# A fused attention and gMLP kernel: a smaller scratch tile in the opening's pool, and GpSimd's sums of weight blocks two column tiles later

## The chip, the cores and the metric

The kernel runs on one core of a Trainium2 chip. The metric is the device time of one execution in microseconds. Engines carry their names in the profile: PE is TensorE, DVE is VectorE, ACT is ScalarE, POOL is GpSimd, SP is SyncE, which here only issues DMAs.

## The reference

One token matrix x of 2048 rows and 512 columns is normalised row by row, and two branches work on the result. All is float32.

```python
xn = _layernorm(x, axis=-1)
s = _A_ref(xn, A_wqkv, A_wo)
g = _silu(_B_ref(xn, B_w_in, B_w_sp, B_b_sp, B_w_out))
return x + s * g
```

Branch A is attention with 32 heads of 16 columns. Each row looks at itself and at seven earlier rows, two apart (window 8, dilation 2), with a softmax over these eight, and the result is multiplied by wo. Branch B is a gMLP: z = gelu(xn @ w_in) with 1792 columns. The second half of z is normalised by row and mixed along the rows by the 2048 x 2048 matrix w_sp, with b_sp added. The result is multiplied by the first half and projected by w_out.

## The kernel before

**Numbers.** TensorE's products are made in fp32r, each operand split into a high and a low part, so one product is three matmuls: high by high, high by low, low by high. A split (`split`, L190 to L193) is an ACT copy for the high part and a DVE subtraction for the low one.

**The opening (L240 to L498).** The product xn @ wqkv is made in three groups of 512 columns, `pair(g, j0)` (L421 to L437) doing two row tiles of 128 at a time: 12 matmuls for a row tile, an ACT copy into a tile `stage`, and from it one store to the DRAM buffer `qkv_d`, 24 stores in all. Group 0 holds the columns that subs 0 and 1 of the attention read, group 2 the last ones. The first six row tiles are transposed by TensorE. Tiles 6 to 15 are fetched already transposed (`fetch_cols`, L255), and a column tile (`column_tile`, L272 to L278) is normalised on DVE by two products (L275) with rows of mean and scale, which come back by DRAM (`rows_out`, `rows_in`: the tile mr), then copied by ACT (L278); `low_x` (L229) makes its low part on DVE. The pow that makes 1/sqrt is on POOL (`rows_ready`, L259 to L262).

**The sums of weight blocks.** Part of the mixing by w_sp uses sums of its blocks. `block_sums` (L389 to L397) loads two tiles of two blocks, adds four times, and stores both tiles to `sums_d`, which the mixing reads much later. Five such sums for the second half are made in the opening by POOL alone, loads, adds and stores (`early_sums`, L410, called at L472 and L473 behind column tile 10 and ahead of column tile 11). Their tiles are t2 tiles. A dependence without a semaphore (NOSYNC, L394) puts their loads behind the last pow in POOL's order.

**Pools of SBUF tiles.** Left of the memory lie whole (the tile BIG), wts, then early (the opening's rows and columns) and, once early is closed, att (the attention's tiles, L513). On the right lie raws, const, then tmp (L88: t2, the stage tiles t35, the tile tz of L350, zpad) and, once tmp is closed (L506), wide (L507: the tiles of the later stages). A pool that is opened on bytes of a closed one waits for the last use of that one.

**The attention (L515 to L664)** works in 16 units: eight subs of four heads, two halves of the rows each. For a unit k, q and v are loaded from `qkv_d` (L536, L537, L545). Two steps per unit are made on DVE: products of q with the eight shifted k (L556), their sums (L563), maximum and shift (L580, L581), an exponential on ACT (L586), the normalisation (L592 to L594), products with v (L600), a first fold on POOL (`first_fold`, L610), two more on DVE (L615, L616), a transpose (L623), and four stores to `o_d` (L626). All have the lowest priority but are chained in their own order.

**The rest** is TensorE's main line: z1 and z2, the two halves of xn @ w_in (L678 to L680, L705 to L707), the mixing g (L795), the projection b by w_out (L1018 to L1020 with the names b), stored to `b_d`, and the attention's projection s by wo (the same lines with the names s), for which `o_d` is loaded (L778) and split. Then the gate is loaded (sg, L1040), goes through silu (L1063), and is multiplied by s (L1073) and added to x (L1075, L1078).

**What sets the order.** The framework's planner lists the instructions of each engine by priority and by its own estimate of when they can run; what `pin` wraps keeps the program's order. Each engine and each issuing queue then goes through its list in order.

Of the kernel before, what the change touches and what calls it, by code (L numbers as in the profile page):

```python
# [11 lines left out]
F32 = mybir.dt.float32  # L12
F32R = mybir.dt.float32r
AF = mybir.ActivationFunctionType
ALU = mybir.AluOpType
AX = mybir.AxisListType

P = 128
S, D, F = 2048, 512, 1792
# [3 lines left out]
NT = S // P  # L23
# [6 lines left out]
HT = NT // 2  # L30
# [21 lines left out]
SYNC = mybir.DependencyInfo(mybir.DependencyClass.Sync, mybir.DependencyReason.DATA)  # L52
NOSYNC = mybir.DependencyInfo(mybir.DependencyClass.NoSync, mybir.DependencyReason.DATA)
# [4 lines left out]
def kernel(  # L58
# [13 lines left out]
    nc = tc.nc  # L72
    pins = [True]

    def pin(ins):
        return tc.keep_in_program_order(ins) if pins[0] else ins
# [12 lines left out]
    tmp = opened.__enter__()  # L89
# [16 lines left out]
    nhalf = raws.tile([P, 1], F32, name="nhalf")  # L106
# [12 lines left out]
    def xn_at(j):  # L119
        return planes[:, FB - KB :, j, 0], planes[:, FB - KB :, j, 1]  # L120
# [22 lines left out]
    def blocks(t, n=KB):  # L143
        return t.rearrange("p (k q) -> p k q", k=n)

    def t2(name, dt=F32, tag="t2", bufs=4):
        return tmp.tile([P, 2 * D], dt, tag=tag, name=name, bufs=bufs)

    def t35(name, dt=F32, wide=False):
        return tmp.tile([P, 2 * GC], dt, tag="t35", name=name, bufs=3)[:, : 2 * GC if wide else FH]  # L150
# [3 lines left out]
    def mm(name):  # L154
        return ps.tile([P, 512], F32, tag=f"bank{next(turn)}", name=name)
# [3 lines left out]
    def weight_pair(name):  # L159
        i = next(slot)  # L160
        return (
            wts.tile([P, 512], F32R, tag=f"whi{i}", name=name + "h"),
            wts.tile([P, 512], F32R, tag=f"wlo{i}", name=name + "l"),
        )

    def fetch(src, n, name):
        raw = raws.tile([P, 512], F32, tag="raw", name=name + "r", bufs=RAW)
        pin(nc.sync.dma_start(raw[:, :n], src))
        return raw
# [25 lines left out]
    def load_x(j):  # L195
        xt = t2(f"x_{j}")[:, :D]
        pin(nc.sync.dma_start(xt, xr[j]))
        return xt

    def stats_x(j, xt):  # L200
        st = const.tile([P, 6], F32, tag="st", name=f"st_{j}", bufs=4)
        pin(nc.vector.bn_stats(st, xt))
        pin(nc.vector.bn_aggr(mvx[:, j], st))
        if j >= JC:
            rstd_x(j)

    def rstd_x(j):
        pin(nc.vector.tensor_scalar(mvx[:, j, 1:2], mvx[:, j, 1:2], EPS, None, op0=ALU.add))
        pin(nc.gpsimd.tensor_tensor(mvx[:, j, 1:2], mvx[:, j, 1:2], nhalf, op=ALU.pow))
# [4 lines left out]
    def normal_x(j, xt):  # L214
        if j < JC:
            pin(nc.vector.tensor_scalar(xt, xt, mvx[:, j, 0:1], None, op0=ALU.subtract))
        else:
            pin(normalise(xt, xt, mvx[:, j]))

    def turned_x(j, xt):  # L220
        pt = mm(f"xt_{j}")
        for i in range(KB):
            pin(nc.tensor.transpose(pt[:, i * P : (i + 1) * P], xt[:, i * P : (i + 1) * P], ident))
        pin(nc.scalar.activation(xn_at(j)[0], blocks(pt), AF.Copy))
        return pt

    def low_x(j, pt):
        hi, lo = xn_at(j)
        pin(nc.vector.tensor_tensor(lo, blocks(pt), hi.bitcast(F32), op=ALU.subtract))  # L229
# [12 lines left out]
    rows = {}  # L242
# [16 lines left out]
    def rows_ready(j0, j1):  # L259
        v = mvx[:, j0:j1, 1]  # L260
        pin(nc.vector.tensor_scalar(v, v, EPS, None, op0=ALU.add))
        return pin(nc.gpsimd.tensor_tensor(v, v, nhalf.to_broadcast([P, j1 - j0]), op=ALU.pow))  # L262

    def rows_in(j0, j1):
        mr = ep.tile([P, 4, 2, P], F32, tag="mr", name=f"mr_{j0}", bufs=2)[:, : j1 - j0]
# [6 lines left out]
    def column_tile(j):  # L272
        xv = cols[j].rearrange("p (k q) -> p k q", k=KB)
        for a, op in ((0, ALU.subtract), (1, ALU.mult)):
            pin(nc.vector.tensor_tensor(  # L275
                xv, xv, rows[j][:, a].unsqueeze(1).to_broadcast([P, KB, P]), op=op
            ))
        pin(nc.scalar.activation(xn_at(j)[0], blocks(cols[j]), AF.Copy))  # L278

    warm = mm("warm")  # L280

# [5 lines left out]
    first = []  # L287

    def opening(wg):
        def high(k):  # L290
            hi, lo = weight_pair(f"wqkv_0_{k}")
            pin(nc.scalar.activation(hi, raw[k], AF.Copy))
            wg[k] = hi, lo

        def low(k, eng):
            pin(eng.tensor_tensor(wg[k][1], raw[k], wg[k][0].bitcast(F32), op=ALU.subtract))

        left = [12, 12]

        def times(j, *kab):  # L300
            for k, a, b in kab:
                pin(nc.tensor.matmul(
                    first[j], xn_at(j)[a][:, k], wg[k][b],
                    start=left[j] == 12, stop=left[j] == 1,
                ))
                left[j] -= 1

        x = [load_x(0)]
        raw = [fetch(wqkv[:, 0, 0, :], GC, "wqkv_0_0")]
        x.append(load_x(1))  # L310
        raw += [fetch(wqkv[:, 0, k, :], GC, f"wqkv_0_{k}") for k in (1, 2)]
        raw.append(t35("wqkv_0_3r")[:, :GC])
        pin(nc.sync.dma_start(raw[3], wqkv[:, 0, 3, :]))
        x.append(load_x(2))
        stats_x(0, x[0])
        high(0)
        normal_x(0, x[0])
        low(0, nc.vector)
        p = turned_x(0, x[0])
        stats_x(1, x[1])  # L320
        low_x(0, p)
        high(1)
        normal_x(1, x[1])
        rstd_x(0)
        low(1, nc.vector)
        high(2)
        low(2, nc.gpsimd)
        keep_warm(2)
        first.append(mm("qkv_0_0"))
        times(0, (0, 0, 0), (0, 0, 1))  # L330
        p = turned_x(1, x[1])
        high(3)
        stats_x(2, x[2])
        low(3, nc.gpsimd)
        times(0, (0, 1, 0), (1, 0, 0), (1, 1, 0), (1, 0, 1), (2, 0, 0), (2, 1, 0))
        low_x(1, p)
        normal_x(2, x[2])
        rstd_x(1)
        first.append(mm("qkv_0_1"))
        times(1, *[(k, 0, 0) for k in range(KB - 1)], (0, 0, 1), (1, 0, 1))  # L340
        times(0, (3, 0, 0), (3, 1, 0), (2, 0, 1))
        p = turned_x(2, x[2])
        times(1, (3, 0, 0), *[(k, 1, 0) for k in range(KB)], (2, 0, 1))
        times(0, (3, 0, 1))
        times(1, (3, 0, 1))
        x += [load_x(j) for j in range(3, OPEN)]
        for j in range(OPEN, OPEN + 4):
            fetch_rows(j)
        raw1 = [fetch(wqkv[:, 1, k, :], GC, f"wqkv_1_{k}") for k in range(3)]
        raw1.append(t2("wqkv_1_3r", tag="tz", bufs=1)[:, :D])  # L350
        pin(nc.sync.dma_start(raw1[3], wqkv[:, 1, 3, :]))
        for j in range(3, OPEN):
            xt = x[j]
            stats_x(j, xt)
            low_x(j - 1, p)
            normal_x(j, xt)
            if j - 1 < JC:
                rstd_x(j - 1)
            first.append(mm(f"qkv_0_{j - 1}"))
            left.append(12)  # L360
            times(j - 1, *[(k, 0, i) for i in range(2) for k in range(KB)])
            p = turned_x(j, xt)
            times(j - 1, *[(k, 1, 0) for k in range(KB)])
            row_stats(OPEN + j - 3)
        low_x(OPEN - 1, p)
        for j in range(10, 13):
            fetch_rows(j)
        for j in range(6, 10):
            fetch_cols(j)
        rows_ready(6, 9)  # L370
        rows_out(6, 9)
        return raw1
# [16 lines left out]
    def block_sums(a, i, tile_=None, eng=nc.vector, loads=nc.sync, stores=nc.scalar):  # L389
        top, low = [(tile_ or t4)(f"s{n}_{a}_{i}") for n in "ab"]  # L390
        for t, r in ((top, 0), (low, HT)):
            ins = loads.dma_start(t, w_sp[2 * a : 2 * a + 2, r + i].rearrange("c p t -> p c t"))
            if tile_:
                tc.add_manual_dep(ins.ins, rows_known.ins.name, NOSYNC, reason="rows first")  # L394
        added([top[:, 0], top[:, 1], low[:, 0], low[:, 1]], eng)
        for r, t in enumerate((top, low)):
            stores.dma_start(sums_d[a, r, i], t)  # L397
# [12 lines left out]
    def early_sums(a, i):  # L410
        block_sums(a, i, early_tile, nc.gpsimd, nc.gpsimd, nc.gpsimd)
# [45 lines left out]
    pair(1, 0)  # L457
    for j in range(13, NT):
        row_stats(j)
    rows_known = rows_ready(13, NT)  # L460
    column_tile(8)
    low_x(7, cols[7])
    fetch_cols(12)
# [5 lines left out]
    column_tile(10)  # L469
    low_x(9, cols[9])  # L470
    pair(1, 4)
    for i in range(HT - 3):  # L472
        early_sums(1, i)  # L473
    for j in range(11, NT):
        if j + 2 < NT:
            fetch_cols(j + 2)
        column_tile(j)
        low_x(j - 1, cols[j - 1])
        if j % 2:
            pair(0, j - 5)  # L480
# [574 lines left out]
    for i in range(0, NT, 2):  # L1055
        j0 = rows_of[i]
# [67 lines left out]
```

## Time and profile before

| what | value |
|---|---|
| median of 3 runs | 753.29 us (751.03 to 753.71) |
| the profiled execution | 751.32 us |
| its span, first to last instruction | 749.5 us |
| PE busy | 697.5 us (93%) |
| DVE busy | 614.3 us (82%) |
| ACT busy | 288.8 us (39%) |
| POOL busy | 154.4 us (21%) |
| mean granted clock of TensorE | 0.967 |

A line of a timeline gives the start, the busy time, the engine and line, the tiles written and read, and in brackets how long the engine had been idle and what released it. PE's matmuls overlap, so their distance counts and not their length. SPq, ACTq are the issuing sides of these engines, and DMA lines are transfers. Tile names are shown without their first numbers.

### The profile page before, as it was taken

How to read it: one execution, taken by the hardware profiler on the slowest of the kernel's cores; microseconds unless marked ns; L12 is line 12 of the kernel's file. 1: busy time of each engine (PE TensorE's matmuls, PEld its weight loads, DVE VectorE, ACT ScalarE, POOL GpSimd, SP SyncE). 2: the span in 40 equal slices, each digit the busy share in tenths (PEclk: the TensorE clock that was granted, in tenths of full speed). 3: DMA queues.
4: the chain of work that ended last, by engine and by line, in shares of the span. 5: the costliest groups of instructions: out<-in, count | busy, mean ns of one | idle time of the engine just before them, and what ended most of it. 6: DMA issues, size and time to landing. Idle time of an engine off the chain costs nothing.

```text
span 749.5 us, 9288 instructions
## 1 busy us (share of the span) xinstructions
PE 697.5 (93%) x3084; PEld 578.8 (77%) x3084; DVE 614.3 (82%) x882; ACT 288.8 (39%) x460; POOL 154.4 (21%) x150
## 2 busy tenths in 40 slices
PE   8989999999999999799999999999999999990474
PEld 7867888888889888588888888888888888880364
DVE  6768310159998999989999999999999999979845
ACT  4422332333424548665345443333434421131222
POOL 3155730000122463421111112111110121221000
PEclk9989999999999999899999999999999999996698
DMA  8798994399998736769997866938778264453568
GB/s 278 224 294 286 297 336 127 102 329 410 363 370 318 234 111 204 224 179 294 373 301 265 277 225 218 313 128 256 234 236 297 74 227 162 164 177 99 151 241 334
DMA packets 109633, 182.38 MB, mean 243 GB/s; under 512 B 10256, under 2 KB 50448, under 8 KB 109584
## 3 DMA queue, kind: packets, MB, share of 16 engines
q1 hardware_dynamic: 66528, 125.55, 50.9%
q10 hardware_dynamic: 40176, 45.75, 17.4%
q0 software_dynamic: 2880, 10.49, 3.9%
q8 instruction: 24, 0.39, 0.2%
q14 instruction: 25, 0.20, 0.1%
HBM read 122.42 MB, written 59.32 MB: 242 GB/s over the span
## 4 chain that ended last, share of the span: by engine, by line
PE 73%; DVE 13%; DMA 8%; issue 2%; ACT 2%; SPq 1%; POOL 0%; DVEq 0%; ACTq 0%
PE g L795 36%; PE qkv L381 4%; PE qkv L380 4%; PE qkv L379 4%; PE z L679 3%; PE z L678 3%; PE z L680 3%; PE z L707 3%; PE z L706 3%; PE z L705 3%; DMA sg<-b_d 3%; DMA ol<-o_d 2%; DVE pr L556 2%; PE b L1019 2%; PE b L1018 2%
## 5 line engine op out<-in xcount | busy, mean ns | idle before, releaser
L610 POOL TENSOR_TENSOR pv<-pv 128x1024 f32<-128x1024 f32 x29 | 69.7, 2403 | 440.4 <-DVE pv L600 440.4
L556 DVE TENSOR_TENSOR pr<-k,q 128x2048 f32<-128x2048 f32 x32 | 73.6, 2299 | 1.3 <-DMA q<-qkv_d 1.2
L600 DVE TENSOR_TENSOR pv<-v,lg 128x2048 f32<-128x2048 f32 x32 | 73.2, 2287 | 0.6
L563 DVE TENSOR_REDUCE lg<-pr 128x128 f32<-128x2048 f32 x32 | 72.9, 2278 | 0.0
L427 ACT ACTIVATE stage<-qkv 128x512 f32<-128x512 f32 x36 | 21.2, 595 | 50.0 <-PE qkv L381 49.9
L1018 PE MATMUL s<-BIG 128*128 128x512 f32 x16 | 7.3, 459 | 27.8 <-ACT BIG L191 27.8
L192 DVE TENSOR_TENSOR w_4l<-w_4r,w_4h 128x512 fp32r<-128x512 f32 x1 | 0.7, 692 | 34.6 <-ACT w_4h L191 34.6
L275 DVE TENSOR_TENSOR xT<-xT,mr 128x512 f32<-128x512 f32 x20 | 18.0, 899 | 11.8 <-DMA mr<-mv_d 9.3
L1029 ACT ACTIVATE bt<-b 128x512 f32<-128x512 f32 x16 | 9.4, 599 | 43.6 <-PE b L1020 39.3
L1018 PEld LDWEIGHTS s<-BIG 128*128 128x128 f32 x16 | 3.5, 220 | 29.0 <-ACT BIG L191 28.3
L707 PE MATMUL z<-w_0h,BIG 128*128 128x512 f32 x64 | 25.0, 391 | 0.0
L706 PE MATMUL z<-w_0l,BIG 128*128 128x512 f32 x64 | 25.0, 391 | 0.0
L705 PE MATMUL z<-w_0h,BIG 128*128 128x512 f32 x64 | 24.9, 389 | 0.0
L726 ACT ACTIVATE zt<-zt,nmz,mvz 128x896 f32<-128x896 f32 x16 | 18.1, 1136 | 11.7 <-POOL nmz L722 11.7
L615 DVE TENSOR_TENSOR pv<-pv 128x512 f32<-128x512 f32 x32 | 21.8, 681 | 0.0
L707 PE MATMUL z<-w_1h,BIG 128*128 128x384 f32 x64 | 21.5, 336 | 0.0
L705 PE MATMUL z<-w_1h,BIG 128*128 128x384 f32 x64 | 21.5, 335 | 0.0
L706 PE MATMUL z<-w_1l,BIG 128*128 128x384 f32 x64 | 21.4, 335 | 0.0
L381 PE MATMUL qkv<-wqkv_0h,BIG 128*128 128x512 f32 x43 | 17.5, 407 | 3.2 <-DVE BIG L229 3.2
L795 PE MATMUL g<-ws_0h,BIG 128*128 128x512 f32 x52 | 20.2, 389 | 0.0
L795 PE MATMUL g<-ws_1h,BIG 128*128 128x512 f32 x52 | 20.2, 389 | 0.0
L795 PE MATMUL g<-ws_2h,BIG 128*128 128x512 f32 x52 | 20.2, 389 | 0.0
(471 smaller groups left out, 2282.8 us busy)
## 6 DMA issues: line engine op xcount, KB each, us to landing
qkv_d<-stage ACTq DMA_DIRECT2D x24, 512.0 KB, 5.0
k<-qkv_d SPq DMA_DIRECT2D x16, 704.0 KB, 5.3
v<-qkv_d SPq DMA_DIRECT2D x16, 704.0 KB, 3.9
z_d<-z1t ACTq DMA_DIRECT2D x14, 512.0 KB
zl<-z_d SPq DMA_DIRECT2D x12, 512.0 KB, 5.9
tr<-t_d SPq DMA_DIRECT2D x12, 384.0 KB, 5.9
x<-in_x SPq DMA_DIRECT2D x16, 256.0 KB, 4.5
sa<-in_w_sp SPq DMA_DIRECT2D x8, 512.0 KB
```

What stands on the lines that cost most here:

```text
L379: nc.tensor.matmul(pq, xh[:, k], wh, start=k == 0, stop=False)
L380: nc.tensor.matmul(pq, xh[:, k], wl, start=False, stop=False)
L381: nc.tensor.matmul(pq, xl[:, k], wh, start=False, stop=k == KB - 1)
L556: line(nc.vector.tensor_tensor(pr, taps(ks[u], j0), qb.unsqueeze(1).to_broadcast([P, W, NJ * CS]), op=ALU.mult))
L563: line(nc.vector.tensor_reduce(lgs[u][:, :, j0 * HS : (j0 + NJ) * HS], pr.rearrange("p w (i d) -> p w i d", d=DH), axis=AX.X, op=ALU.add,))
L600: line(nc.vector.tensor_tensor(pv.rearrange("p w (i d) -> p w i d", d=DH), taps(vs[u], j0).rearrange("p w (i d) -> p w i d", d=DH), lgs[u] ...
L610: eng.tensor_tensor(pv[:, 0:4], pv[:, 0:4], pv[:, 4:8], op=ALU.add)
L705: nc.tensor.matmul(pz, xh[:, k], wh, start=k == 0, stop=False)
L706: nc.tensor.matmul(pz, xh[:, k], wl, start=False, stop=False)
L707: nc.tensor.matmul(pz, xl[:, k], wh, start=False, stop=k == KB - 1)
L795: nc.tensor.matmul(pg, z[a], w[b], start=start and i == 0, stop=stop and i == 2, skip_group_check=seeded)
L1018: nc.tensor.matmul(pp[:, cols], hi, wh, start=k == 0, stop=False)
```

## The change

The helper `t2` takes a width, and the tile tz takes half of the bytes it had. The sums' loop moves from ahead of column tile 11 to behind column tile 12, and its loads wait by a semaphore (SYNC) for the last DVE product of that column tile instead of standing behind the pow. `rows_ready` and `column_tile` are changed only in what they return.

```diff
-    def t2(name, dt=F32, tag="t2", bufs=4):
-        return tmp.tile([P, 2 * D], dt, tag=tag, name=name, bufs=bufs)
+    def t2(name, n=2, tag="t2", bufs=4):
+        return tmp.tile([P, n * D], F32, tag=tag, name=name, bufs=bufs)
...
     def column_tile(j):
         xv = cols[j].rearrange("p (k q) -> p k q", k=KB)
         for a, op in ((0, ALU.subtract), (1, ALU.mult)):
-            pin(nc.vector.tensor_tensor(
+            done = pin(nc.vector.tensor_tensor(
                 xv, xv, rows[j][:, a].unsqueeze(1).to_broadcast([P, KB, P]), op=op
             ))
         pin(nc.scalar.activation(xn_at(j)[0], blocks(cols[j]), AF.Copy))
+        return done
...
-        raw1.append(t2("wqkv_1_3r", tag="tz", bufs=1)[:, :D])
+        raw1.append(t2("wqkv_1_3r", 1, tag="tz", bufs=1))
...
             if tile_:
-                tc.add_manual_dep(ins.ins, rows_known.ins.name, NOSYNC, reason="rows first")
+                tc.add_manual_dep(ins.ins, turned.ins.name, SYNC, reason="columns first")
...
-    for i in range(HT - 3):
-        early_sums(1, i)
     for j in range(11, NT):
         if j + 2 < NT:
             fetch_cols(j + 2)
-        column_tile(j)
+        turned = column_tile(j)
+        if j == 12:
+            for i in range(HT - 3):
+                early_sums(1, i)
         low_x(j - 1, cols[j - 1])
```

More of the change, by code (lines that the diff above doesn't have):

```diff
@@ L261, in rows_ready @@
         pin(nc.vector.tensor_scalar(v, v, EPS, None, op0=ALU.add))
-        return pin(nc.gpsimd.tensor_tensor(v, v, nhalf.to_broadcast([P, j1 - j0]), op=ALU.pow))
+        pin(nc.gpsimd.tensor_tensor(v, v, nhalf.to_broadcast([P, j1 - j0]), op=ALU.pow))
     def rows_in(j0, j1):
@@ L459 @@
         row_stats(j)
-    rows_known = rows_ready(13, NT)
+    rows_ready(13, NT)
     column_tile(8)
```

## The prediction

> **What bounds the kernel now.** First the page: the span, and the strips of PE and DVE in 40 slices of 18.7 us.
>
> ```profile
> span 749.5 us, 9288 instructions
> ...
> PE   8989999999999999799999999999999999990474
> DVE  6768310159998999989999999999999999979845
> ```
>
> PE is full from slice 8 to slice 35 and nearly empty in slice 36. DVE shows the reverse: it is nearly idle in slices 5 to 7 and full until the end. So DVE, which has all of the attention, begins late and finishes late, and PE pays at the end. To price both places I cut the span into stretches (us, then busy time of PE, PEld, DVE, ACT, POOL, each with its count, then clock and DMA):
>
> ```profile
> 41.00:50.00 9.00, 8.47 (x38) 6.68 (x36) 1.85 (x5) 2.32 (x4) 3.51 (x5) 1.00 0.94 297
> 50.00:66.00 16.00, 13.55 (x46) 10.50 (x46) 15.90 (x11) 4.55 (x8) 14.17 (x12) 0.79 0.74 254
> 92.00:163.00 71.00, 71.00 (x315) 58.80 (x314) 8.98 (x13) 21.91 (x35) 6.18 (x6) 1.00 0.66 212
> 163.00:715.20 552.20, 519.38 (x2309) 433.23 (x2308) 528.69 (x745) 225.90 (x361) 104.01 (x93) 0.97 0.71 239
> ```
>
> DVE works 9.0 of the 71 us before 163 and 528.7 of the 552.2 after it. The other end is PE's order of instructions, then the chain of work that ended last:
>
> ```profile
> 658.00 0.39 PE L1020 MATMUL b<-wout_6h,BIG 128*128 128x512 f32 x1
> 658.23 0.39 PE L1018 MATMUL s<-BIG 128*128 128x512 f32 x1
> ...
> 702.54 0.79 PE L1018 MATMUL s<-BIG 128*128 128x512 f32 x1 [27.84 <-ACT BIG L191]
> ```
>
> ```profile
> 714.65 0.46 DVE tt L623
> ...
> 716.45 1.58 DMA o_d<-tt
> ```
>
> PE finishes the gMLP's last product b at 658.4 and goes on with s, the attention's output projection. It then stands 27.84 us for an operand that comes by DRAM from the attention's transposes (L623), the last of which ends at 715.1. From there to the end of the span are 34.4 us. So **the attention's end on DVE bounds the kernel**, and the question is what makes the attention begin at 163. The order on ACT and SP, and the first attention product:
>
> ```profile
> 86.26 0.37 ACTq L436 DMA_DIRECT2D qkv_d<-stage  x1
> ```
> ```profile
> 148.81 0.38 ACTq L436 DMA_DIRECT2D qkv_d<-stage  x1
> ...
> 153.92 1.28 ACT L687 ACT_TABLE_LOAD   x1 [3.03 <-DMA qkv_d<-stage]
> ```
> ```profile
> 153.97 0.38 SPq L392 DMA_DIRECT2D sa<-in_w_sp  x1
> ...
> 154.92 0.46 SPq L536 DMA_DIRECT2D k<-qkv_d  x1
> ```
> ```profile
> 163.07 2.29 DVE L556 TENSOR_TENSOR pr<-k,q 128x2048 f32<-128x2048 f32 x1 [0.96 <-DMA q<-qkv_d]
> ```
> ```profile
> qkv_d<-stage ACTq DMA_DIRECT2D x24, 512.0 KB, 5.0
> k<-qkv_d SPq DMA_DIRECT2D x16, 704.0 KB, 5.3
> ```
>
> The twelfth of the 24 stores from stage, at 86.26, is the last of column group 0, and units 0 to 3 of the attention read only that group. Its k could be fetched from about 91 (86.3 and the 5.0 us that these stores take to land, in the page's DMA rows). It is fetched at 154.9, one microsecond after the last store of all, of group 2, has landed (ACT is released at 153.9). What ties the two is in the layout: tmp, which holds the stage tiles, and att, which holds k and q, share bytes. Adding up the tiles in the code, from the bottom: 1,024 bytes of scratch, 128 of constants, BIG 114,816, wts 36,864, which puts att at 152,832; its k, q, three lg, pr, mx, v, sm, pv and tt are 34,048, so it ends at 186,880. From the top, 229,376: raws 8,256, const 1,344, tmp 33,024, so tmp begins at 186,752. The overlap is 128 bytes, of tt with zpad, and a pool that takes another's bytes waits for that pool as a whole. The row of sa shows it: its bytes in wide were last used by a tile of POOL's sums, whose stores are issued by 105 (below), and yet it goes out at 153.97, together with the end of the last store from stage.
>
> **The change part by part.** *The tile tz* shrinks from 4 KB to 2 KB (its upper half was never used), so tmp begins at 188,800 and no longer touches att. No instruction goes or comes. att now waits only for early, whose last reader is the low half of column tile 15 (the end of the first row below), and for group 0's stores.
>
> ```profile
> 74.16 1.48 DVE L229 TENSOR_TENSOR BIG<-xT,BIG 128x512 fp32r<-128x512 f32 x2
> 84.74 1.67 DVE L192 TENSOR_TENSOR wqkv_0l<-wqkv_0r,wqkv_0h 128x512 fp32r<-128x512 f32 x1 [9.11 <-ACT wqkv_0h L191]
> ```
>
> Where the wait goes, the next thing late is group 0's last store: 86.3, less about 5 us for the opening below, then 5 us to land, 1 us of issue and 5.3 us for k and q: the first product at about 93 instead of 163. Beside it PE runs the products of groups 1 and 2, which need DVE only for the four splits that begin at 84.74, and DVE has 62 of 71 us free there.
>
> *The sums of weight blocks* (five on POOL, each two loads, four adds, two stores) move from behind column tile 10 to behind column tile 12, and their loads now wait for that tile's second product on DVE, where before they only stood behind the last pow in POOL's order.
>
> ```profile
> 41.36 0.96 POOL L392 DMA_DIRECT2D sa<-in_w_sp  x1
> ...
> 53.56 1.61 POOL L387 TENSOR_TENSOR sa<-sa,sb 128x512 f32<-128x512 f32 x1
> ...
> 104.08 0.56 POOL L397 DMA_DIRECT2D sums_d<-sb  x1
> ...
> 193.40 2.40 POOL L610 TENSOR_TENSOR pv<-pv 128x1024 f32<-128x1024 f32 x1 [88.77 <-DVE pv L600]
> ```
> ```profile
> 35.51 1.37 DVE L275 TENSOR_TENSOR xT<-xT,mr 128x512 f32<-128x512 f32 x2
> ...
> 52.27 3.45 DVE L275 TENSOR_TENSOR xT<-xT,mr 128x512 f32<-128x512 f32 x2
> ```
> ```profile
> 29.27 4.68 DMA mr<-mv_d
> ...
> 42.57 6.66 DMA mr<-mv_d
> ```
>
> Beside POOL's adds two column products take 3.45 us instead of 1.37, and the row fetch beside the four loads of 41 to 48 takes 6.66 instead of 4.68. A column tile (three such operations) then costs DVE 5.2 us, while PE's twelve matmuls for it take 12 x 0.227 = 2.7 (0.227 is the distance of the starts at 658.00 and 658.23). That is why PE does 38 + 46 matmuls, 19.1 us of work, in the 25 us from 41 to 66. Without the adds a tile costs about 2.1 us, below PE's pace, and mr lands 2 us sooner. The bounds are nothing and all 5.9 us; I take 5, because a first wait for mr stays. Column tile 12 should end near 57, so the sums run from 57 to about 121 instead of 41 to 105, with all 20 of their DMAs. Queued behind the new wait on POOL is nothing until the attention's folds (L610), the first of which now wants POOL some 22 to 30 us after the first product (193.4 - 163.1 = 30 now, with other work between), so from 115 on. SP's queue is not touched, as these loads are POOL's own. Nobody reads the sums before
>
> ```profile
> L795 PE MATMUL g<-ws_0h,BIG x52: 389/389/389, 397.1 to 568.9; 128*128 128x512 f32 x52
> ```
>
> What is new is the neighbour: some twelve of the 20 adds (those after 92 when shifted by 15 us) now meet the attention's two-input products. Priced by the column products it is (3.45 - 1.37)/2 = 1.04 us each, 12 us together; at nothing if the planner puts them beside the one-input L563, at 20 x 1.6 = 32 us if every add of POOL stops DVE for its whole length. I take 12.
>
> **The sum.** Does the attention end in time?
>
> ```profile
> 665.63 0.69 DVE L192 TENSOR_TENSOR o_0l<-ol,o_0h 128x512 fp32r<-128x512 f32 x1 [3.90 <-ACT o_0h L191]
> ```
>
> DVE's 528.7 us of 163 to 715.2 hold 11 such splits of o, 7.6 us, that belong to the projection; 521 remain. To them come the 9 us from 92 to 163, the idle 23.5 us less the 3.9 of this row, 12 beside POOL, and 8 at the start for loads that a single k and q tile cannot run ahead (my estimate: five units by the 1 to 2 us that a load of 5.3 outlasts the operations beside it): 93 + 521 + 9 + 20 + 12 + 8 = 663. It has to end by 668 (below), so **PE is the bound**, though narrowly. The rows for the end, DVE's last products and PE's small stops between the groups of s:
>
> ```profile
> 743.76 1.35 DVE L1073 TENSOR_TENSOR sg<-s,sg 128x512 f32<-128x512 f32 x3 [2.34 <-ACT sg L1063]
> ```
> ```profile
> 708.41 0.50 PE L1018 MATMUL s<-BIG,o_0h 128*128 128x512 f32 x1 [0.83 <-DVE sg L1073]
> ...
> 721.17 0.50 PE L1018 MATMUL s<-BIG,o_3h 128*128 128x512 f32 x1 [1.59 <-ACT o_3h L191]
> ...
> 726.60 0.50 PE L1018 MATMUL s<-BIG,o_0h 128*128 128x512 f32 x1 [2.42 <-DVE sg L1073]
> ```
>
> - b ends at 658.4 - 5 = 653.4;
> - s is 15 rows of 12 matmuls at 0.227 and 24 half-wide ones at about half, 0.12: 43.7 us, so 697.1;
> - from the start of DVE's last products to the end of the span 749.5 - 743.8 = 5.7, as now: 702.8;
> - the small stops, 4.84 us now, stay with 4: 706.8.
>
> The span comes to about 707. The profiled execution took 751.32 us around a span of 749.5, 1.8 more, so **709 us**; that execution lies within the runs shown (751.03 to 753.71, median 753.29).
>
> **Rivals.** *The attention's end still binds.* POOL's program has the sums ahead of the folds, so the first fold may wait until they are done near 121, and DVE's order stands behind it. Then the attention gains 28 us less and ends at 682; with the 34.4 that follow it today the span is 716, the time 718. For it: the fold is the only thing that links DVE to POOL, and the adds are long. Against: only the first units can meet it. It decides from an attention end of 703 - 34.4 = 668. If still more is lost, up to 735.
>
> *The change does not do what it says*: k waits for the last stage store for another reason, such as its place on SP behind the loads sa and sb, which need tmp's bytes. The row at 154.92, right behind them, would look the same. Then only the opening's 5 us are left: 744.5, a time of 746. Against: k belongs to another pool than sa, and o_d is read from 659.6 on while it is still written at 716, so a DRAM buffer is not waited for as a whole:
>
> ```profile
> 659.64 5.52 SPq L778 DMA_DIRECT2D ol<-o_d  x7
> ```
>
> *Slower: the sums hold the next pool.* The sums' tiles lie in tmp, and wide, which takes tmp's bytes, cannot open before the last sum is stored. PE begins the z1 products at 148.0,
>
> ```profile
> L678 PE MATMUL z<-BIG,w_0h x16: 389/389/389, 148.0 to 158.2; 128*128 128x512 f32 x16
> ```
>
> and its eight banks last 8 x 2.7 = 22 us, so a release after 170 stops PE microsecond for microsecond. The 42 us gained are then eaten, and the time passes 755, from a release at about 216, when the sums take 159 us instead of 64. For it: they now run beside an almost full DVE. Against: POOL's fold takes 2.40 us in the middle of the attention, and an issue costs the same beside a busy DVE as beside an idle one:
>
> ```profile
> 43.05 0.73 POOL L392 DMA_DIRECT2D sa<-in_w_sp  x1
> ...
> 63.54 0.73 POOL L392 DMA_DIRECT2D sa<-in_w_sp  x1 [1.32 <-DMA sums_d<-sa]
> ```
>
> The Trainium skill, "SBUF — State Buffer", section "SBUF: two separate sides", speaks for this rival: it warns that DMAs issued from the GpSimd queue can starve, as their descriptors are written through a port pair that VectorE's two-port operations lock. By it each of the 20 DMAs could wait for an operation of the attention; the two rows do not show such a wait.
>
> **How the numbers follow.** Forecast, PE bound, 700 to 716: 66%. Attention's end binds, 716 to 735: 15%. No effect on the attention, 744 to 748: 8%, half of it within 0.5% (some 3.8 us, about what a measurement of this kernel can tell from no change). Slower: 8%, with 757 as its middle. Still below 700, if the 4 us of stops and the stall near 300 go too: 3%. Leaving out the last three, 19%, the range is 700 to 735. Faster 0.66 + 0.15 + 0.04 + 0.03 = 0.88, same 0.04, slower 0.08.
>
> **What would show it.** Right: the first L556 near 93 with k's issue far ahead of the last store from stage; column products of 0.7 us each between 47 and 57; the last L623 before 668; no idle of PE above 5 us between b and s. Wrong: k still behind sa (second rival); a first fold that starts only when POOL's last L397 is out (first); ACT's first L687 far later than 154 (third).

## The result and the profile after

The changed kernel takes 721.1 us (median of 4 runs, 718.98 to 723.11), the kernel before 752.2 (750.59 to 753.71) on the same chip. The ratio is 0.959, with a 95% interval of 0.955 to 0.962. That is faster, inside the range of 700 to 735, and 12 us above the predicted 709. The profiled execution took 718.98 us around a span of 717.2. Lines behind the first edit are one or two higher than before (L556 is L558, L623 is L625, L795 is L797). The page of the changed kernel, its span and four strips:

```profile
span 717.2 us, 9264 instructions
...
PE   8999999999999999668999999999999999999997
...
DVE  6774668989999998979989998899999999980464
...
PEclk9999999999999999867999999999999999999999
```

The empty slice 36 of PE is gone, DVE no longer idles in slices 4 to 7, and it has time to spare at the end. New is a hole in PE in slices 16 to 18, with a lower clock. The stages of PE's main line, read from PE's order of instructions as the start of each stage's first matmul (us):

| | opening, to z | z, to g | g, to b | b, to s | s, to its last matmul | to the end of the span |
|---|---|---|---|---|---|---|
| before | 148.0 | 153.4 | 280.7 | 76.1 | 81.4 | 9.9 |
| after | 140.9 | 153.5 | 298.7 | 76.1 | 43.9 | 4.1 |
| difference | -7.1 | +0.1 | **+18.0** | 0 | -37.5 | -5.8 |

The differences add up to -32.3, the two spans differ by 32.3. The change gained 50 us and lost 18 in the stage g, the mixing by w_sp. First what was gained. Windows of the opening and of the stretch behind it (columns as before: busy time and count of PE, PEld, DVE, ACT, POOL, then clock, DMA share, GB/s):

```profile
41.00:50.00 9.00, 9.00 (x41) 7.46 (x40) 4.78 (x10) 3.62 (x7) 0.06 (x1) 1.00 0.71 217
50.00:66.00 16.00, 16.00 (x72) 13.21 (x71) 10.25 (x16) 6.17 (x12) 4.56 (x5) 1.00 0.94 307
92.00:163.00 71.00, 71.00 (x315) 58.82 (x314) 59.88 (x67) 22.88 (x38) 30.72 (x22) 1.00 0.94 316
```

PE makes 113 matmuls in 41 to 66 where it made 84, without a stop. POOL, busy for 17.7 us of these 25 before, now works 4.6. DVE's own timeline shows the column products, two in a row:

```profile
45.95 1.42 DVE L275 TENSOR_TENSOR xT<-xT,mr 128x512 f32<-128x512 f32 x2 [4.15 <-DMA mr<-mv_d]
...
60.39 1.41 DVE L275 TENSOR_TENSOR xT<-xT,mr 128x512 f32<-128x512 f32 x2
```

Each costs 0.7 us, and none is stretched to half of 3.45 any more. Between 92 and 163 DVE is busy 59.9 us instead of 9.0: the attention runs. SP's queue, ACT's stores and DVE's first product show where it begins:

```profile
75.46 0.33 SPq L538 DMA_DIRECT2D k<-qkv_d  x1
```
```profile
71.95 0.37 ACTq L437 DMA_DIRECT2D qkv_d<-stage  x1
...
76.48 0.37 ACTq L437 DMA_DIRECT2D qkv_d<-stage  x1
```
```profile
80.49 2.29 DVE L558 TENSOR_TENSOR pr<-k,q 128x2048 f32<-128x2048 f32 x1 [0.31 <-DMA k<-qkv_d]
```

The first k goes out ahead of the store at 76.48, the twelfth, and not behind the last of 24. The other end, on DVE (the attention's last transpose) and on PE (from b to s, and the last matmul):

```profile
642.35 0.45 DVE L625 STREAM_TRANSPOSE tt<-pv 128x256 f32<-128x256 f32 x1
```
```profile
669.00 0.39 PE L1022 MATMUL b<-wout_6h,BIG 128*128 128x512 f32 x1
669.23 0.39 PE L1020 MATMUL s<-BIG 128*128 128x512 f32 x1
...
712.78 0.28 PE L1022 MATMUL s<-BIG,o_3l 128*128 128x256 f32 x1
```

The attention is done 26 us ahead of s, and s runs through. Now what was lost. PE's timeline from the last matmul of z2, with every stop between z and b:

```profile
294.21 0.33 PE L709 MATMUL z<-w_1h,BIG 128*128 128x384 f32 x1
...
300.50 0.80 PE L940 MATMUL g<-wsp_0h,BIG 128*128 128x512 f32 x1 [5.03 <-ACT zt L710]
...
304.31 0.80 PE L797 MATMUL g<-wsp_0h,BIG 128*128 128x512 f32 x1 [1.21 <-ACT g L815]
...
309.68 0.79 PE L940 MATMUL g<-wsp_0h,BIG 128*128 128x512 f32 x1 [2.44 <-ACT zt L710]
...
322.21 1.75 PE L797 MATMUL g<-wsp_3h,BIG 128*128 128x512 f32 x4 [3.71 <-ACT wsp_3h L191]
...
327.47 0.79 PE L797 MATMUL g<-wsp_3l,BIG 128*128 128x512 f32 x1 [3.51 <-DVE wsp_3l L192]
```

Five stops, 15.9 us, where the kernel before had two, 3.43 and 0.72. The first and third wait for L710, ACT's eviction of z2 products, because g needs their PSUM banks. The other two long ones wait for the split of the fourth block of w_sp. ACT's timeline has both causes:

```profile
308.65 0.98 ACT L710 ACTIVATE zt<-z 128x512 f32<-128x512 f32 x2 [3.32 <-DMA t_d<-zt]
...
317.58 1.64 ACT L815 ACTIVATE g<-b_bh 128x512 f32<-128x512 f32 x3 [4.37 <-DMA b_bh<-in_b_sp]
...
321.54 0.61 ACT L191 ACTIVATE wsp_3h<-wsp_3r 128x512 fp32r<-128x512 f32 x1
```

The last eviction of z2 ends at 309.6, **15.1 us after PE made the product** (294.5). And wsp_3h stands on ACT behind copies of b_bh (L815), which wait 4.37 us for their load. Below, "late" is this lateness of z2's last eviction, and "stops" the sum of PE's stops in g.

### The profile page after: what moved, and what is told of

It reads as the page before. It is cut to its first block, busy times and chain, and to the rows that moved or that the text cites. A ratio compares the mean times of both kernels' runs of the same rounds, so it can differ in the third digit from the quotient of the medians.

```text
span 717.2 us, 9264 instructions
## 1 busy us (share of the span) xinstructions
PE 694.8 (97%) x3084; PEld 577.4 (81%) x3084; DVE 608.0 (85%) x882; ACT 284.6 (40%) x458; POOL 159.0 (22%) x150
## 4 chain that ended last, share of the span: by engine, by line
PE 89%; DMA 3%; DVE 3%; issue 1%; POOL 1%; ACT 1%; SPq 0%; ACTq 0%; DVEq 0%
PE g L797 37%; PE qkv L380 5%; PE qkv L381 5%; PE qkv L382 5%; PE z L680 4%; PE b L1021 4%; PE z L681 4%; PE b L1020 4%; PE b L1022 4%; PE z L682 4%; PE z L709 2%; PE z L708 2%; PE z L707 2%; PE s L1021 2%; PE s L1020 2%; PE s L1022 2%
## 5 line engine op out<-in xcount | busy, mean ns | idle before, releaser
L612 POOL TENSOR_TENSOR pv<-pv 128x1024 f32<-128x1024 f32 x29 | 71.8, 2474 | 344.2 <-DVE pv L602 344.2
L558 DVE TENSOR_TENSOR pr<-k,q 128x2048 f32<-128x2048 f32 x32 | 74.5, 2327 | 6.7 <-DMA q<-qkv_d 6.3
L728 ACT ACTIVATE zt<-zt,nmz,mvz 128x896 f32<-128x896 f32 x16 | 18.1, 1134 | 21.9 <-POOL nmz L724 20.5
L1075 DVE TENSOR_TENSOR sg<-s,sg 128x512 f32<-128x512 f32 (+1 forms) x17 | 11.2, 658 | 16.9 <-PE s L1022 16.1
L191 ACT ACTIVATE BIG<-zl 128x512 fp32r<-128x512 f32 x20 | 12.5, 629 | 30.7 <-DVE zl L862 30.6
L275 DVE TENSOR_TENSOR xT<-xT,mr 128x512 f32<-128x512 f32 x20 | 13.8, 688 | 11.3 <-DMA mr<-mv_d 6.4
L192 DVE TENSOR_TENSOR BIG<-zt,BIG 128x512 fp32r<-128x512 f32 (+2 forms) x24 | 19.5, 825 | 3.0 <-ACT BIG L191 3.0
L192 DVE TENSOR_TENSOR o_1l<-ol,o_1h 128x512 fp32r<-128x512 f32 x3 | 2.1, 689 | 23.2 <-ACT o_1h L191 23.2
L797 PE MATMUL g<-ws_0h,BIG 128*128 128x512 f32 x52 | 20.2, 389 | 0.0
L797 PE MATMUL g<-ws_1h,BIG 128*128 128x512 f32 x52 | 20.2, 389 | 0.0
L797 PE MATMUL g<-ws_3h,BIG 128*128 128x512 f32 x52 | 20.2, 389 | 0.0
```

Of the source, the lines that this page charges most:

```text
L558: line(nc.vector.tensor_tensor(pr, taps(ks[u], j0), qb.unsqueeze(1).to_broadcast([P, W, NJ * CS]), op=ALU.mult))
L612: eng.tensor_tensor(pv[:, 0:4], pv[:, 0:4], pv[:, 4:8], op=ALU.add)
L797: nc.tensor.matmul(pg, z[a], w[b], start=start and i == 0, stop=stop and i == 2, skip_group_check=seeded)
```

## The experiments

The first four take the change apart. Each was run in 4 runs beside the kernel before.

**tz_only**: the smaller tile, the sums in their old place.

```diff
-        raw1.append(t2("wqkv_1_3r", tag="tz", bufs=1)[:, :D])
+        raw1.append(tmp.tile([P, D], F32, tag="tz", name="wqkv_1_3r", bufs=1))
```

> Only the tile tz is halved; the sums stay where they were. If the shared bytes alone held the attention back (my theory), its first product comes near 93 instead of 163, PE's wait of 27.8 us before s is gone, and only the opening's 7 us are missing against the changed kernel: about 728 us. If the moved sums carry a large part of the gain (rival), it stays above 735.

708.25 us (707.2 to 709.64), ratio 0.944 [0.942, 0.947]. One tile's 2 KB brings 42 us, more than the whole change and 20 more than expected. The opening lasts 147.6 us (148.0 before), the attention's first product comes at 100.8, and PE has a single stop in g (its timeline):

```profile
309.87 0.80 PE L795 MATMUL g<-wsp_1l,BIG 128*128 128x512 f32 x1 [3.76 <-DVE wsp_1l L192]
```

z2 is evicted 1.0 us late, and g takes 280.3 us. So the 18 us are not the price of a free attention as such.

**zpad_early**: the 4 KB of tz stay. Instead the pad's tile goes from the pool tmp to early, and its two stores go up behind its memset.

```diff
-    zpad = tmp.tile([PAD, CS], F32, tag="zpad", name="zpad", bufs=1)
+    zpad = ep.tile([PAD, CS], F32, tag="zpad", name="zpad", bufs=1)
     nc.vector.memset(zpad, 0.0)
+    for t in (1, 2):
+        nc.sync.dma_start(
...
```

> tz keeps its 4 KB and the sums their place; only zpad (256 bytes at tmp's lower end) lives in the pool early instead, so tmp and att no longer share the 128 bytes. If the overlap is the cause (my theory), the time is that of the kernel with the smaller tz alone, about 728 us. If the size of tz or what is done with it matters (rival), nothing changes: 752.

711.1 us (709.13 to 712.11), ratio 0.947 [0.944, 0.950]; the first product comes at 103.1. The same gain with another edit: what held the attention was the 128 bytes that the two pools shared. The 3 us against tz_only stand in the opening, which ends 3.3 us later.

**sums_only**: the sums behind column tile 12, tz with its 4 KB.

```diff
-        raw1.append(t2("wqkv_1_3r", 1, tag="tz", bufs=1))
+        raw1.append(t2("wqkv_1_3r", 2, tag="tz", bufs=1)[:, :D])
```

> Only the sums move; tz keeps 4 KB. My theory: the column tiles are quick, z1 begins 7 us earlier, the last store from stage with it, and the attention still begins behind that store, near 156: 745 us. Rival: the sums' place moves the attention by itself, 735 or less.

743.7 us (742.1 to 745.48), ratio 0.991 [0.988, 0.994]. The opening gains 7 us here too (z begins at 141.1), g is not longer (279.1), and the old stop stands ahead of s, in PE's timeline:

```profile
693.97 0.80 PE L1020 MATMUL s<-BIG 128*128 128x512 f32 x1 [27.70 <-ACT BIG L191]
```

The parts do not add: -42 and -7 alone, -31 together. Once the attention is free, the move of the sums costs 13 us: g takes 18.4 us more than in tz_only, and the opening gives 6.7 of them back.

**seeds_third**: the changed kernel, with the loads of b_bh and its copies two block pairs later in the program, to take wsp_3 out from behind them.

```diff
-        steps=([second_seeds], [], [], []),
+        steps=([], [], [second_seeds], []),
```

> The changed kernel, and the loads and copies of the second bias (second_seeds) come two block pairs later in the program, so that ACT splits the blocks 3 and 4 of w_sp ahead of the copies that wait for that load, as it did before the change. If the 18 us that PE loses anew at the start of g come from the planner's order there (theory A), about 8 us come back: 713. If DVE is simply behind because attention and z2 together fill it (theory B), the wait only changes its name: 719 to 722.

717.3 us (711.63 to 719.22), ratio 0.955 [0.950, 0.959], not to be told from the changed kernel. The stops at wsp_3 go, but z2 gets one of 3.55 us, and g still has 10.8 us of them (late: 14.4). The order at the seam, where z2 ends and g begins, is at best a part of it by itself.

The next four ask what makes ACT late. Theory B says DVE's time, theory P POOL's four small operations per tile between DVE's statistics (L719, L720) and ACT's normalization (L728), theory C the accident of where the attention's products fall.

**hold11**: the attention is written as a generator and stops ahead of its step 11 (of 32); from there on it stands behind the last `bn_aggr` of z2 (`counted`, sent in behind the loop over z2) in DVE's order.

```diff
         for i, (u, j0) in enumerate(steps):
+            if i == 11:
...
+                held = yield
...
+                last.append(held)
...
-    attention()
+    waiting = attention()
+    next(waiting)
...
+    waiting.send(counted)
```

> The changed kernel, with the attention's step 11 of 32 and all later ones held, in DVE's order only, behind the last statistics of z2; nothing else differs. In the changed kernel the last eviction of z2 comes 15.1 us after its product, and the first product of g to its last takes 298.8 us; with the smaller tile alone it is 1.0 us and 280.4 us. Theory B (the attention's products stand in DVE's queue ahead of the statistics and splits of z2, and ACT falls behind): the last eviction at most 6 us late, g about 283 us, the time 705 to 710 us. Theory P (it is POOL's small operations between DVE's statistics and ACT's normalization that are stretched beside DVE's long products): one product fewer there, so half of it at most, 711 to 717 us. If neither: 719 to 723 us.

**700.05 us** (697.38 to 703.3), ratio 0.933 [0.929, 0.937]. That is 5 us better than theory B had it. z2 is 4.7 us late, g takes 275.4, and what is left of the stops of g in PE's timeline is

```profile
301.86 0.50 PE L808 MATMUL g<-wsp_1l,BIG 128*128 128x512 f32 x1 [0.31 <-DVE wsp_1l L192]
...
311.22 0.50 PE L808 MATMUL g<-wsp_4l,BIG 128*128 128x512 f32 x1 [0.91 <-DVE wsp_4l L192]
```

The attention still ends at 641.1: what it lost beside z2 it made up while PE worked on g.

**two_tiny** and **tz_two_tiny**: two of POOL's four small operations go to DVE, in the changed kernel and in tz_only.

```diff
-        nc.gpsimd.tensor_tensor(nm, mv[:, 0:1], mone, op=ALU.mult)
-        nc.gpsimd.tensor_scalar(mv[:, 1:2], mv[:, 1:2], EPS, None, op0=ALU.add)
+        nc.vector.tensor_tensor(nm, mv[:, 0:1], mone, op=ALU.mult)
+        nc.vector.tensor_scalar(mv[:, 1:2], mv[:, 1:2], EPS, None, op0=ALU.add)
```

> The changed kernel, with two of POOL's four small operations per tile of z2 (the sign of the mean and the addition of EPS) moved to DVE, so that POOL has two, not four, in the chain between the statistics and the normalization. Theory P: the waits of ACT for POOL in 262 to 312, 12.0 us in the changed kernel, fall to about half, the last eviction comes 8 us late or less instead of 15.1, the time 708 to 714 us. Theory B: DVE has 32 more small operations, and the time stays at 719 to 724 us.

718.75 us (716.55 to 720.25), ratio 0.958 [0.954, 0.962]. ACT's waits for POOL in 262 to 312, total, number and longest, first in the changed kernel, then in two_tiny:

```profile
ACT zt L728 <- POOL nmz L724: 12.0, 5, 5.1
```
```profile
ACT zt L728 <- POOL nmz L724: 11.2, 2, 8.3
```

Half of the operations, and nearly as much waiting (late: 13.7). Theory P, as it was put, falls.

> The smaller tile alone (the sums in their old place), with the same two small operations of POOL per tile of z2 moved to DVE. It was 708.25 us without that move. Theory P: the waits of ACT for POOL in 262 to 312, 10.0 us there, fall to about half; what stop is left at the start of g, 3.8 us, may go: 704 to 708 us. Theory B: 708 to 710 us.

713.35 us (712.72 to 713.56), ratio 0.950 [0.948, 0.953]: 5 us slower than tz_only, which neither theory had. z2 is 14.1 us late instead of 1.0. With 32 more small operations on DVE, the good order of tz_only tips over. DVE's timelines show where: in tz_only the attention's last product of q and k (L556) ahead of the end of z2 stands at 303.20, behind 30 of the 32 `bn_stats` of z2; here it stands at 301.74, behind 26 of them, as in the changed kernel (300.27).

**sums11**: the changed kernel, with the sums behind column tile 11.

```diff
-        if j == 12:
+        if j == 11:
```

> The changed kernel with POOL's sums behind column tile 11 instead of 12: the same work, and the attention starting a little earlier or later. Theories B and P by themselves: no change, 718 to 723 us, as both causes stay. Theory C (what counts is where the attention's long products happen to fall in DVE's order against the last tiles of z2, which any shift of the start moves): the time changes by more than 5 us one way or the other, and the lateness of the last eviction of z2 with it.

720.1 us (715.73 to 720.3), ratio 0.958 [0.954, 0.962]. The attention begins at 90.4 instead of 80.5, and z2 is 14.6 us late all the same. The opening loses 4.7 us (its last column products are stretched again), and g is 8.6 us shorter (290.1), while z2 has a stop of 3.0. A shift by 10 us alone does not cure it. That any shift of the start moves the products' places, as theory C had it, is not so: their last two (L558) ahead of the end of z2 stand behind 20 and 26 of the 32 `bn_stats` in both kernels. Whether those places are what counts, this run does not test.

The last four test hold11 itself.

**hold12**: meant as a control. The hold stands at step 12, which I took to have its place behind the last statistics of z2 in any case.

```diff
-            if i == 11:
+            if i == 12:
```

> A control for hold11: the same code, but the hold stands one step later, at step 12, which in the changed kernel stands behind z2's last statistics on DVE anyway. Step 11 stays where it was, behind 26 of the 32 statistics. Theory B (it is the attention's work on DVE beside z2): back to the changed kernel, 717 to 723 us, g near 295 us, the last eviction of z2 12 us late or more. If the gain of hold11 came from how the attention is written into the program, and not from DVE's time: 698 to 704 us.

708.2 us (706.85 to 710.63), ratio 0.943 [0.941, 0.946]. That lies between the two expectations, and it is no control. A step begins with the product of q and k (L558) for the step three further on, and behind it come two folds of the step before. In the changed kernel this part of step 12, 3.4 us of DVE, stands ahead of the last of z2's statistics; only its later part stands behind them. DVE's timeline, in the changed kernel and in hold12:

```profile
300.27 2.28 DVE L558 TENSOR_TENSOR pr<-k,q 128x2048 f32<-128x2048 f32 x1
...
314.32 0.19 DVE L720 BATCH_NORM_AGGREGATE mvz<-zst 128x2 f32<-128x12 f32 x1
```
```profile
313.40 0.20 DVE L728 BATCH_NORM_AGGREGATE mvz<-zst 128x2 f32<-128x12 f32 x1
313.51 2.24 DVE L558 TENSOR_TENSOR pr<-k,q 128x2048 f32<-128x2048 f32 x1
```

So of the 21 us that hold11 gained on the changed kernel, 13 come when the first part of step 12 leaves z2, and 8 more when step 11 leaves it too. z2 is still 13.3 us late. What differs as well is the order at the seam, here on SP and on ACT:

```profile
309.22 0.33 SPq L168 DMA_DIRECT2D wsp_3r<-in_w_sp  x1
312.66 0.33 SPq L948 DMA_DIRECT2D b_bl<-in_b_sp  x1
```
```profile
312.57 0.63 ACT L191 ACTIVATE wsp_3h<-wsp_3r 128x512 fp32r<-128x512 f32 x1
...
316.78 2.16 ACT L826 ACTIVATE g<-b_bh 128x512 f32<-128x512 f32 x4 [2.74 <-DMA b_bh<-in_b_sp]
```

and in the changed kernel on SP:

```profile
311.43 0.33 SPq L937 DMA_DIRECT2D b_bl<-in_b_sp  x1
...
313.37 0.38 SPq L168 DMA_DIRECT2D wsp_3r<-in_w_sp  x1
```

There wsp_3 stood behind b_bl and b_bh in both lists, and PE stopped 3.71 and 3.51 us for it. In hold12 the planner lists wsp_3 first, and PE's stops in g are 8.2 us instead of 15.9, the longest being that for the late eviction:

```profile
303.57 0.79 PE L951 MATMUL g<-wsp_0h,BIG 128*128 128x512 f32 x1 [5.87 <-ACT zt L718]
```

This order by itself does not make the stops. In tz_only b_bl and b_bh stand ahead of wsp_3 on SP too (304.98 and 305.36, then 309.17), and on its ACT

```profile
310.62 2.14 ACT L813 ACTIVATE g<-b_bh 128x512 f32<-128x512 f32 x4
...
316.05 0.62 ACT L191 ACTIVATE wsp_3h<-wsp_3r 128x512 fp32r<-128x512 f32 x1
```

but PE does not stop for wsp_3 there. The copies come 7 us earlier than in the changed kernel and do not wait for their load.

**hold11_load**: hold11, with four DVE products that nothing reads in the place of step 11.

```diff
+            if i == 6:
+                for n in range(4):
+                    load = ap_.tile([P, W, NJ * CS], F32, tag="pr", name=f"load_{n}")
+                    nc.vector.tensor_tensor(
...
```

> hold11 (700.05 us) with four products of 128x2048 on DVE, some 9 us, that nothing reads, put behind 17, 18, 22 and 22 of the 32 statistics of z2, about the DVE time of the step that hold11 keeps out; no loads, no folds, no ACT work with them. Theory B in its strict form (only DVE's time counts): the last eviction of z2 is again 10 us late or more, g 285 us or more, the time 710 to 720 us. If the step costs by its loads, its fold on POOL or its table loads on ACT: 700 to 703 us.

712.1 us (711.88 to 713.02), ratio 0.948 [0.947, 0.950]. The four products in the groups by line, and the longest stop of PE:

```profile
L785 DVE TENSOR_TENSOR load<-b_a 128x2048 f32<-128x2048 f32 x4 | 9.1, 2263 | 0.0
```
```profile
306.76 0.79 PE L961 MATMUL g<-wsp_0h,BIG 128*128 128x512 f32 x1 [3.79 <-ACT zt L718]
```

9.1 us of DVE, with no loads, folds or ACT work of their own, make z2 9.4 us late (10 or more expected), bring 7.8 us of stops and cost 12 us. So DVE's time counts in this place. It did not change alone, though: on SP b_bl now stands ahead of wsp_3 (311.07 and 312.00), where hold11 has wsp_3 first (300.17 and 300.59). Of the stops, 5.8 us wait for z2's evictions and 2.0 for wsp_3h.

**hold10** and **tz_hold10**: the hold one step earlier, in hold11 and in tz_only (there it is its step 10, and the first product of its step 11, that stood ahead of the last statistics).

```diff
-            if i == 11:
+            if i == 10:
```

> hold11 with the hold one step earlier, so that two steps of the attention, 10 and 11, are kept out of z2. Theory B: the last eviction of z2 is 3 us late or less, but g had no stop worth a microsecond left in hold11 (0.31 and 0.91 us), so g stays at 274 to 276 us and the time at 698 to 703 us; the attention's last transpose, 641 in hold11, comes some 10 us later, still ahead of s.

700.8 us (698.36 to 702.21), ratio 0.932 [0.930, 0.934]. g has no stop and takes 272.9 us, although z2 is 6.1 us late (3 or less expected). But the attention now ends at 659.7, s stops twice (0.52 and 1.39 us) and lasts 46.3 instead of 43.9.

> The smaller tile alone (the sums in their old place), with its step 10, which there stands behind 24 of the 32 statistics of z2, and all later ones held behind the last of them. It was 708.25 us without the hold, g 280.4 us. Theory B: g 275 to 277 us as in hold11, the time 703 to 705 us, so that the move of the sums is again worth about what it was worth alone to the kernel before (7 us of opening), less what starts later. If the move of the sums is bad beside the free attention for another reason: 700 us or less.

701.35 us (700.11 to 701.78), ratio 0.933 [0.932, 0.935]; g takes 272.9 again, with no stop, 2 us less than expected (z2 is 1.7 us late). The three best kernels, one of them without the move of the sums, cannot be told apart. In hold10, 2.6 us of its shorter opening are lost in a stop at the beginning of z2, 2.5 in s, 2.3 behind s: held until z2 ends, the attention starts again at the same time as in tz_hold10 (its next product at 307.2 in both) and ends no sooner (659.7 and 658.8).

## Why the prediction was right, and where it missed

*What gates the attention*: right. Two different edits that part att from tmp each free it (tz_only, zpad_early). The first product came at 80.5, not 93. I had waited for the wrong store: by the order of the calls of `pair`, group 0 ends with the eleventh store, `pair(0, 14)`, and the twelfth belongs to group 1. The eleventh went out at 83.60 in the kernel before and goes out at 71.95 now, so the opening gave 11.7 us at this place and not 5. The first k goes out 3.5 us behind it, at 75.46, released by a store from stage.

*The sums*: right, 7.1 us of opening instead of 5, more than the 5.9 that I had given as the most. PE has no stop left from 41 to 66, where I kept 0.9 us for the wait for mr; DVE still waits 4.15 us for it. They run from 54.6 to 123.4 (57 to 121 predicted), and POOL's timeline shows the rivals' signs in small:

```profile
54.63 0.96 POOL L393 DMA_DIRECT2D sa<-in_w_sp  x1 [13.58 <-DVE BIG L229]
...
98.05 3.22 POOL L388 TENSOR_TENSOR sa<-sa,sb 128x512 f32<-128x512 f32 x1
101.36 0.75 POOL L393 DMA_DIRECT2D sa<-in_w_sp  x1
...
116.66 4.44 POOL L612 TENSOR_TENSOR pv<-pv 128x1024 f32<-128x1024 f32 x1
...
122.84 0.56 POOL L398 DMA_DIRECT2D sums_d<-sb  x1
```

The first fold stands between the adds, not behind the last store, and takes 4.44 us; it delays DVE by 2.3 us. An issue costs 0.75 us beside the attention, as before: the starving of such DMAs that the Trainium skill warns of ("SBUF — State Buffer", section "SBUF: two separate sides") is not seen in this trace, and the wide pool opens without a delay of z.

*Does the attention end in time*: right, and by more than the 5 us I gave it. The last transpose ends at 642.8, not 663. The start came 12.5 us earlier, which leaves 8 of these 20 us for the allowances for the adds and the loads (20 us together), as too high. *The end*: s takes 43.9 us (43.7), with no small stops (4), and 4.1 us come behind its last matmul (5.7). None of the rivals took place. The time of 721 misses the forecast for a kernel bound by PE, 700 to 716. It lies where I had put the first rival, but the attention's end does not bind; that the range of 700 to 735 holds it is luck.

*The step that failed* is the first of the sum, "b ends at 658.4 - 5": it carries the whole main line from the opening to b along as a block. The opening gave more, but g grew by 18.0 us, and b ended at 669.2. The terms that I had written come to 707 - 2.1 (opening) - 4 (stops) - 1.6 (end) = 699, and with 18 to 717, the span. I read the stall near 300 of the kernel before as a fixed 4 us that might only go, and did not ask what the freed attention would do to the order of the engines' lists there.

What the runs show of these 18 us is the following.

- DVE work ahead of z2's last statistics goes with late evictions and with lost time. With the first part of step 12 held out of z2 the kernel gained 13 us (hold12), with step 11 too 8 more (hold11), and 9.1 us of bare DVE work in the place of step 11 cost 12 (hold11_load). One way from DVE to ACT is in the row at 308.65 above: the last eviction waits 3.32 us for the transfer t_d<-zt, which sends off what DVE's combinations (L741) made of an earlier tile and so frees it.
- A full DVE is not enough to cause it. From 262 to 300 DVE is busy 37.2 us in the kernel before, 35.9 in the changed one and 38.0 in tz_only, where z2 is 1.0 us late. Nor is all lateness lost time: in hold10 z2 is 6.1 us late without a stop in g, and in the kernel before 8.0 without a stop for it.
- The order of DVE's list goes with the lateness, though not always. The last product of q and k ahead of the end of z2 stands behind 26 of the 32 `bn_stats` in the changed kernel, seeds_third, two_tiny, sums11 and tz_two_tiny (13.7 to 15.1 us late), and behind 30 in tz_only and zpad_early (1.0 and 1.8). But it stands behind 26 in the kernel before and in sums_only as well (8.0 and 6.5), and in hold12 the last one stands behind 20, and z2 is 13.3 us late.
- wsp_3 behind the bias copies makes 7.2 us of the stops in the changed kernel. The same order stands in tz_only without a stop for wsp_3, and seeds_third, which undoes it, gained 4 us at most, within the noise.

How the 18 us divide between DVE's time and the order of the lists is not shown, since the edits that change the one changed the other. Why the move of the sums makes the planner choose the worse order, when neither POOL nor the opening reaches into that stage, stays open.

## What to carry to other kernels

When a gate falls and a long chain of work moves by 60 us, look at each stage that it will now share with the main line on its engine, and at the order of the lists at each seam: a stage that merely kept up before can become late without one instruction being added. Parts of a change that gain alone need not add; run each alone. A control counts as one only when the trace shows that it moved nothing: the first part of step 12 stood elsewhere than its number said. A chain that has time to spare at its end can be held out of the one stage where the main line needs its engine (700 us here instead of 721).

## What the runs showed of the hardware

A stop of PE costs more than its length. The granted clock in stretches of 4 us of the changed kernel, columns as above, the clock third from the end:

```profile
300.00:304.00 4.00, 2.59 (x5) 1.41 (x5) 4.00 (x5) 3.61 (x8) 2.52 (x2) 0.50 0.29 82
...
316.00:320.00 4.00, 2.51 (x12) 1.73 (x10) 2.16 (x5) 2.42 (x5) 0.00 (x0) 1.00 0.92 320
...
328.00:332.00 4.00, 4.00 (x11) 3.06 (x10) 4.00 (x8) 1.06 (x2) 0.00 (x0) 0.50 0.76 225
```

and over 300 to 340 in the changed kernel and in hold10:

```profile
300.00:340.00 40.00, 28.63 (x84) 20.86 (x85) 36.02 (x61) 22.48 (x38) 9.51 (x15) 0.67 0.61 196
```
```profile
300.00:340.00 40.00, 40.00 (x179) 33.10 (x177) 38.33 (x59) 24.01 (x40) 11.49 (x10) 1.00 0.64 213
```

From 328 to 332 PE is busy all the time and makes 11 matmuls, where 4 us hold 18 at 0.227 each. Against the 272.9 us of g without a stop, 15.9 us of stops cost 25.8 in the changed kernel, 8.2 cost 12.9 in hold12, 3.76 cost 7.4 in tz_only, and 7.0 cost 10.4 in tz_two_tiny: between 1.5 and 2 times their length. The clock does not account for all of it: in hold11, where it stays at 1.00 from 300 to 340, 1.2 us of stops go with 2.5 more in g. The Trainium skill ("TensorE: Matmul & The Clock Gate", section "Part 1: The HAM clock gate") says that an idle window of about 3.4 us halves the clock until PE has been busy for as long; the 0.50 behind the stop of 5.03 us agrees. In sums_only a shorter stop was enough: behind 1.88 us, ending at 298.88, the granted clock is 0.52 from 299 to 302 and 0.50 from 302 to 306.
